# Bucketed attention with a gated feed-forward: the stacked score operands are assembled by compute engines in place of transfers

## The chip, the cores and the metric

The kernel runs on one core of a Trainium2 chip. Time is what the device takes for one execution, in microseconds (us). A core has five engines with a queue each: PE multiplies matrices, DVE, ACT and POOL work on tiles in SBUF (DVE and ACT on PSUM too), SP here only issues transfers. Transfers run on 16 DMA engines; each is issued by an instruction in the queue of SP or ACT, and a queue is worked off in order. The program is built by a scheduler that takes a priority from the kernel's own counter (`at(g, k)`), draws the waits from the tiles, and fixes the order on each engine before anything runs.

## The reference

Four batches with eight heads of 768 positions and 64 channels go through attention in which a query sees only the keys of its own hash bucket (six sign bits of a projection); a gated feed-forward layer over each batch follows.

```python
q_bits = (np.einsum('bhsd,dk->bhsk', q, proj) > 0)      # k_bits alike, from k
q_bucket = np.sum(q_bits * 2 ** np.arange(6), axis=-1)
mask = q_bucket[:, :, :, None] == k_bucket[:, :, None, :]
scores = np.where(mask, np.matmul(q, k.transpose(0, 1, 3, 2)) / 8, -1e9)
attn = softmax(scores);  x = attn @ v
# per batch, x is 768 x 512
h = np.maximum(x @ w_in, 0);  u, v = h[..., :512], h[..., 512:]
v_n = (v - mean(v)) / np.sqrt(var(v) + 1e-6)
out = (u * (w_spatial @ v_n + b_spatial[:, None])) @ w_out
```

## The kernel before, in words

There are 32 heads (n = 0 to 31), handled in pairs (p = n // 2, e = n % 2): a pair's q and k are one tile `qk` of 128 rows, of which head e has rows 64e to 64e + 63. To keep float32's accuracy with float16 matmuls each operand is split into a rounded part and a remainder. `split_qk` makes the tile `hl` (128 x 4 x 768, float16): slot 1 and 2 are the rounded k and q (ACT, line 186), slot 0 and 3 the remainders (DVE, lines 187 and 188). `hash_rows` multiplies q and k with the projection and turns the signs into rows of plus and minus a large number, `sg` (DVE, lines 178 and 180); multiplied with each other these rows add a large negative number to a score whose buckets differ.

A score tile (128 queries by 768 keys, `sp`) is then two matmuls of up to 128 rows for each half of the keys, lines 300 and 301. Their operands are stacked in `ab`, one of four tiles of 128 x 4 x 768 that the heads take in turn: rows 0 to 63 hold the head's parts, rows 64 to 127 the other parts in slots 0 and 1, and the hash rows with zeros in slots 2 and 3. Putting `ab` together is `build(n)`, lines 191 to 217. Since a head's rows have to come to other rows than where `hl` and `sg` hold them, it issues transfers from SBUF to SBUF: four small ones of hash rows (line 203), and one or two of 192 or 384 KB from `hl` (lines 201, 207, 216, 217). For heads 8 to 31 (`near`) two copies by DVE that stay on their rows (lines 209 and 210) stand for part of it, and the four small transfers are issued from ACT's queue.

The main loop runs over g = 6n + i, six score tiles a head. For heads 0 and 8 to 31 a tile goes: matmuls (lines 300 and 301), a pass of DVE that also takes the row maximum (302), ACT's exponent (303, 304), a split of the result into two float16 parts `pp` (ACT 307, DVE or POOL 308), a transposing transfer `pt` issued by SP (310), and 18 matmuls with v (323 to 325), five tiles later. For heads 1 to 7 (`KEYS`) the scores are made with keys and queries exchanged (`scores_k`, lines 269 to 272), which needs the row maxima first (`row_max`, lines 248 to 261) and no transfer per tile; in that time the feed-forward weights are loaded and split too. When the heads of a batch are done, its feed-forward layer is spread over the heads of the next batch in 28 units (lines 372 to 448); the last batch's stands alone at the end.

`build(n + 2)` is called at tile i = 0 of head n. `split_qk(r + 2)` comes at tile 3 of an odd head, where r is the pair that runs; there is one `hl` tile and one `qk` tile at a time, so the next split waits for whatever still reads `hl`, and the next load of `qk` for the split.

## Time and profile before

| | |
|---|---|
| median of 3 runs | 709.54 us (708.9 to 712.29) |
| the profiled execution | 708.95 us, of which its span is 707.2 us |
| granted TensorE clock, mean | 0.964 |
| busy share of the span | PE 87%, DVE 72%, ACT 64%, POOL 31% |
| DMA, mean share of 16 engines | 78%, 111.51 MB moved |

The span is read in five stages: until the first score matmul (0 to 16.5 us), head 0 (to 62), the KEYS heads 1 to 7 (to 175), heads 8 to 31 with the feed-forward layers of three batches (to 632, called the long stage), and the last feed-forward layer (to 707.2). In the profile's rows a name such as `ab<-hl` is output and input of an instruction, `SPq` and `ACTq` are the queues of SP and ACT where they issue transfers, and what stands behind `<-` in brackets is what ended the engine's idle time.

### The profile page before, as it was taken

How to read it: one execution, taken by the hardware profiler on the slowest of the kernel's cores; microseconds unless marked ns; L12 is line 12 of the kernel's file. 1: busy time of each engine (PE TensorE's matmuls, PEld its weight loads, DVE VectorE, ACT ScalarE, POOL GpSimd, SP SyncE). 2: the span in 40 equal slices, each digit the busy share in tenths (PEclk: the TensorE clock that was granted, in tenths of full speed). 3: DMA queues.
4: the chain of work that ended last, by engine and by line, in shares of the span. 5: the costliest groups of instructions: out<-in, count | busy, mean ns of one | idle time of the engine just before them, and what ended most of it. 6: DMA issues, size and time to landing. Idle time of an engine off the chain costs nothing.

```text
span 707.2 us, 14858 instructions
## 1 busy us (share of the span) xinstructions
PE 618.5 (87%) x5735; PEld 391.0 (55%) x5735; DVE 511.3 (72%) x961; ACT 454.2 (64%) x806; POOL 222.0 (31%) x215
## 2 busy tenths in 40 slices
PE   1668798999796989999796999899888999999997
PEld 0236676778453655565454565565445655655553
DVE  4665698388888897779699897899697987725100
ACT  1444477567686868777588786868677688724121
POOL 5111434454324452152002162033022530322513
PEclk9999798699899999999998999999999999999999
DMA  9557557353698979998989999999989899950011
GB/s 242 143 109 185 125 154 161 89 163 106 134 185 176 184 161 199 217 194 192 206 153 214 165 197 191 201 185 215 214 171 151 158 180 206 156 132 1 0 45 45
DMA packets 286555, 111.51 MB, mean 158 GB/s; under 512 B 270356, under 2 KB 273428, under 8 KB 286484
## 3 DMA queue, kind: packets, MB, share of 16 engines
q1 hardware_dynamic: 284180, 109.67, 77.0%
q10 hardware_dynamic: 2304, 0.89, 0.6%
q8 instruction: 45, 0.74, 0.4%
q14 instruction: 26, 0.21, 0.1%
HBM read 28.33 MB, written 6.29 MB: 49 GB/s over the span
## 4 chain that ended last, share of the span: by engine, by line
PE 48%; DMA 22%; DVE 11%; issue 7%; SPq 4%; ACT 4%; POOL 4%; ACTq 0%; DVEq 0%; POOLq 0%
DMA pt<-pp 14%; PE sps L428 7%; PE ops L443 7%; PE vps L372 6%; PE ups L413 6%; PE pv L282 4%; DMA ab<-hl 4%; PE sp L300 3%; PE sp L301 3%; PE pv L323 3%; SPq L310 2%; PE pv L325 2%; PE pv L324 2%; DVE ex L302 2%; PE sp L269 1%
## 5 line engine op out<-in xcount | busy, mean ns | idle before, releaser
L302 DVE TENSOR_SCALAR_CACHE_REDUCE ex<-sp 128x768 f32<-128x768 f32 x150 | 141.8, 951 | 42.1 <-PE sp L301 39.7
L304 ACT ACTIVATE ex<-ex,nb 128x768 f32<-128x768 f32 x150 | 139.3, 932 | 7.4 <-ACT nb L303 4.5
L323 PE MATMUL pv<-vp,pt 128*128 128x65 f16 x900 | 105.7, 196 | 43.3 <-DMA pt<-pp 42.7
L307 ACT CAST pp<-ex 128x768 f16<-128x768 f32 x150 | 123.7, 826 | 10.5 <-DMA pt<-pp 5.2
L308 DVE TENSOR_TENSOR pp<-ex,pp 128x768 f16<-128x768 f32 x116 | 123.1, 1064 | 9.5 <-ACT pp L307 8.9
L308 POOL TENSOR_TENSOR pp<-ex,pp 128x768 f16<-128x768 f32 x34 | 57.9, 1702 | 218.0 <-ACT pp L307 175.3
L323 PEld LDWEIGHTS <-pt 128*128 128x128 f16 x900 | 85.5, 100 | 70.7 <-DMA pt<-pp 61.8
L300 PE MATMUL sp<-ab 128*128 128x384 f16 x300 | 102.1, 340 | 14.4 <-DMA ab<-hl 9.3
L324 PE MATMUL pv<-vp,pt 128*128 128x64 f16 x900 | 105.4, 196 | 0.0
L325 PE MATMUL pv<-vp,pt 128*128 128x65 f16 x900 | 104.8, 197 | 0.0
L301 PE MATMUL sp<-ab 127*128 127x384 f16 (+1 forms) x300 | 102.2, 341 | 0.6 <-DMA ab<-sg 0.6
L428 PE MATMUL sps<-ws,vn 128*128 128x384 f16 x576 | 100.7, 326 | 0.5 <-DVE sy L432 0.5
L324 PEld LDWEIGHTS <-pt 128*128 128x128 f16 x900 | 85.9, 99 | 10.7 <-issue 1.9
L325 PEld LDWEIGHTS <-pt 128*128 128x128 f16 x900 | 86.0, 99 | 2.3 <-issue 0.6
L428 PEld LDWEIGHTS <-vn 128*128 128x128 f16 x576 | 54.3, 98 | 35.1 <-issue 1.8
L282 PEld LDWEIGHTS pv<-vf,ex 128*128 128x128 f32 x504 | 69.2, 210 | 3.2 <-issue 1.0
L372 PE MATMUL vps<-wi,xt 128*128 128x512 f16 x288 | 67.4, 382 | 3.2 <-DMA xt<-xs 3.2
L413 PE MATMUL ups<-xt,wi 128*128 128x384 f16 x384 | 69.4, 333 | 0.0
L443 PE MATMUL ops<-wo,g 128*128 128x512 f16 x288 | 67.8, 379 | 1.0 <-ACT o L447 0.9
L282 PE MATMUL pv<-vf,ex 128*128 128x65 f32 x504 | 68.0, 289 | 0.0
L303 ACT ACTIVATE nb<-mx 128x1 f32<-128x1 f32 x150 | 29.3, 197 | 57.2 <-DVE ex L302 56.2
L433 POOL TENSOR_TENSOR sy<-sy,u 128x384 f32<-128x384 f32 x32 | 35.9, 1125 | 75.5 <-DVE sy L432 54.5
(91 smaller groups left out, 920.8 us busy)
## 6 DMA issues: line engine op xcount, KB each, us to landing
qk<-kq SPq DMA_DIRECT2D x16, 768.0 KB
ab<-hl SPq DMA_DIRECT2D x34, 192.0 KB
out<-o SPq DMA_DIRECT2D x24, 256.0 KB
v<-v SPq DMA_DIRECT2D x13, 384.0 KB
raw<-w_in SPq DMA_DIRECT2D x16, 256.0 KB
ab<-hl SPq DMA_DIRECT2D x7, 384.0 KB
pt<-pp SPq DMA_TRANSPOSE x150
raw<-w_sp SPq DMA_DIRECT2D x12, 192.0 KB
```

What stands on the lines that cost most here:

```text
L282: nc.tensor.matmul(acc[:, qi, :], lhsT=ex[:, qi * P:(qi + 1) * P], rhs=vf[p % 2][:, 2 * i + e, :], start=(i == 0 and qi == 0), stop=(i == ...
L300: nc.tensor.matmul(ps[:, c], lhsT=t[:, 0, qs], rhs=t[:, 1, cs], start=True, stop=False)
L301: nc.tensor.matmul(ps[:, c], lhsT=t[0:K, 3, qs], rhs=t[0:K, 2, cs], start=False, stop=True)
L302: nc.vector.tensor_scalar(ex, ps, -float(2 ** 28), None, op0=ALU.max, op1=ALU.max, accum_out=mx)
L304: st["ex", n, i] = nc.scalar.activation(ex, ex, AF.Exp, bias=nb, scale=ISQ).ins
L307: nc.scalar.copy(pp[:, 0], ex)
L308: (nc.gpsimd if i in (PL_POOL if n >= 2 * NH else PL_POOL1) else nc.vector).tensor_tensor(out=pp[:, 1], in0=ex, in1=pp[:, 0], op=ALU.subtract)
L323: nc.tensor.matmul(acc, lhsT=pt[:, c, :], rhs=vh, start=(i == 0 and c == 0), stop=False)
L324: nc.tensor.matmul(acc[:, 0:D], lhsT=pt[:, c, :], rhs=vl, start=False, stop=False)
L325: nc.tensor.matmul(acc, lhsT=pt[:, NT + c, :], rhs=vh, start=False, stop=(i == NT - 1 and c == NT - 1))
L428: nc.tensor.matmul(ps[:, :HS], lhsT=vn[gv][:, c, d * P:(d + 1) * P], rhs=ws[gw][:, c, hs], start=(k == 0), stop=(k == 3 * NT - 1))
L443: nc.tensor.matmul(ps, lhsT=gt[h][gg][:, c, j * P:(j + 1) * P], rhs=wo[gw][:, c, :], start=(k == 0), stop=(k == 3 * NF - 1))
```

## The change

All transfers in `build` go. `build(n)` now returns four steps, which the loop runs one after the other:

- `codes`: four instructions that take 32 rows of `sg` each, multiply them with a column `hm` of 0 or the head's factor, and write them to rows 64 to 95 of `ab`; two by ACT and two by DVE (head 0: four by ACT). The rows of the pair's other head come along and are zeroed by the factor, so the separate scaling in `hash_rows` (line 180) goes.
- `high` and `cross`: copies of 64 x 1536 float16 from `hl` to rows 0 to 63 and 64 to 127. The one that stays on its rows is POOL's, the one that crosses to the other half DVE's (head 0: ACT and DVE).
- `low`: a third copy of that size, by DVE.

For heads 2 to 7 all four run at tile 0 of head n - 2, for heads 8 to 31 one at each of tiles 0 to 3. At the start `hm` is made from a small tile `hw`, head 1's operands follow head 0's, head 1's row maxima are spread over tiles 0 to 3 of head 0 (so far five came ahead at tile 0 and one at tile 1), and some loads are placed in another order. Heads 9, 11 and so on now stack as the even heads do, with 127 rows in line 301's matmul.

```diff
+    hw = const.tile([P, 2, 4], F32, name="hw")
+    nc.gpsimd.memset(hw, 1.0)
+    nc.gpsimd.affine_select(out=hw, in_=hw, compare_op=ALU.is_ge, fill=0.0, base=0,
+                            pattern=[[-16, 2], [-32, 4]], channel_multiplier=1)
+    nc.gpsimd.affine_select(out=hw, in_=hw, compare_op=ALU.is_ge, fill=0.0, base=15,
+                            pattern=[[16, 2], [32, 4]], channel_multiplier=-1)
...
-        s0 = wk.tile([P, HS], F16, tag="sg0", name=f"sg0_{p}")
+        s0 = wk.tile([P, HS], F16, tag="sg0", bufs=2, name=f"sg0_{p}")
         nc.vector.tensor_scalar(s0, hp[:, :HS], 0.0, hv[:, 0:1], op0=ALU.is_gt, op1=ALU.subtract)
-        s1 = wk.tile([P, HS], F16, tag="sg1", bufs=2, name=f"sg1_{p}")
-        nc.vector.tensor_scalar(s1, s0, hv[:, 1:2], None, op0=ALU.mult)
-        st["sg", p] = s1
+        st["sg", p] = s0
...
-        for j in range(4):
-            q_s.dma_start(
-                out=t[z:z + 2 * NB, 3 - j // 2, (j % 2) * HS:(j % 2 + 1) * HS],
-                in_=sg[32 * j + 16 * e:32 * j + 16 * e + 2 * NB, :])
...
-        q_h.dma_start(out=t[z:z + D, 0:2], in_=hl[r, 2:4])
+        def codes():
+            for j in range(4):
+                js, hs = slice(32 * j, 32 * j + 32), slice((j % 2) * HS, (j % 2 + 1) * HS)
+                to = t[D:D + 32, 3 - j // 2, hs]
+                if j < 2 or n == 0:
+                    st["code"] = nc.scalar.activation(to, sg[js], AF.Copy, scale=hm[js, e:e + 1]).ins
+                else:
+                    nc.vector.tensor_scalar(to, sg[js], hm[js, e:e + 1], None, op0=ALU.mult)
+
+        def high():
+            if n == 0:
+                nc.scalar.copy(t[0:D, 2:4], hl[r, 1:3])
+            else:
+                OWN[e].tensor_copy(t[0:D, 2:4], hl[r, 1:3])
+
+        def low():
+            nc.vector.tensor_copy(t[0:D, 0:2], hl[r, 0:2])
+
+        def cross():
+            eng = nc.vector if n == 0 else OWN[1 - e]
+            st["cross"] = eng.tensor_copy(t[D:P, 0:2], hl[r, 2:4]).ins
+
+        return [codes, high, low, cross]
+
+    OWN = (nc.gpsimd, nc.vector)
...
     nc.sync.dma_start(out=hc, in_=hconst)
     load_qk(0)
+    nc.vector.reduce_sum(hm, hw, axis=AX.X)
+    nc.vector.tensor_scalar(hm, hm, hv[:, 1:2], None, op0=ALU.mult)
     hash_rows(0)
+    at(-40, 1)
     split_qk(0)
-    build(0)
+    at(-39, 0)
+    for part in build(0):
+        part()
+    load_v(0)
+    at(-38, 0)
     load_qk(1)
-    build(1)
-    load_v(0)
+    at(0, 150)
+    first = st["cross"], st["code"]
+    with tc.issue_after(first[0]), tc.issue_after(first[1]):
+        for part in build(1):
+            part()
...
-    rml = [(NT * n + i - NT - LEAD, n, i) for n in sorted(KEYS) for i in range(NT)]
+    rml = [((0, 1, 2, 2, 3, 3)[i] if n == 1 else NT * n + i - NT - LEAD, n, i) for n in sorted(KEYS) for i in range(NT)]
...
-            if i == BI and n + 2 < N:
-                build(n + 2)
+            if i == 0 and n + 2 < N:
+                parts = build(n + 2)
+            for part in parts[:1] if n + 2 >= NH else parts:
+                part()
+                parts = parts[1:]
```

Where the order on an engine moved is shown below at three places. A row is a line of the kernel, an operation, output and input with their numbers, and the output's size.

SP's queue from the start of the program to the first transposing transfer of head 0 (`pt_0`), before the change (`ab_82` is head 0's operand tile, `ab_83` head 1's, `ab_85` head 3's):

```order
L216 DMA ab_83<-hl_121 64x2x1536
L217 DMA ab_82<-hl_121 64x1536
L150 DMA qk_132<-kq 128x1536
L217 DMA ab_83<-hl_121 64x1536
L203 DMA ab_82<-sg_0_119 12x384 x4
L203 DMA ab_83<-sg_0_119 12x384 x4
L156 DMA v_4_1201<-v 128x768
L216 DMA ab_85<-hl_167 64x2x1536
L150 DMA qk_173<-kq 128x1536
L203 DMA ab_85<-sg_1_165 12x384 x4
L217 DMA ab_85<-hl_167 64x1536
L310 DMA_TRANSPOSE pt_0_156<-pp_0_153 128x12x128
```

The same stretch of SP's queue with the change (lines are numbered higher by 7 or 8 there, and L505 on is the start):

```order
L131 DMA bt<-b_sp 128x768
L157 DMA qk_139<-kq 128x1536
L163 DMA v_4_1207<-v 128x768
L157 DMA qk_177<-kq 128x1536
L318 DMA_TRANSPOSE pt_0_162<-pp_0_159 128x12x128
L318 DMA_TRANSPOSE pt_1_205<-pp_1_202 128x12x128
```

Only loads are left ahead of `pt_0`; SP holds 270 rows in place of 322, and ACT issues no transfer any more.

DVE's queue from the signs of pair 0 to head 0's first score tiles (`ex_0`, `ex_1`), before:

```order
L178 TENSOR_SCALAR sg_0_117<-hp_112,hc 128x384
L224 SCALAR_TENSOR_TENSOR vp_94<-v_0_140,vp_94 128x12x64
L180 TENSOR_SCALAR sg_0_119<-sg_0_117,hc 128x384
L178 TENSOR_SCALAR sg_1_163<-hp_158,hc 128x384
L187 SCALAR_TENSOR_TENSOR hl_167<-qk_132,hl_167 128x768
L188 SCALAR_TENSOR_TENSOR hl_167<-qk_132,hl_167 128x768
L180 TENSOR_SCALAR sg_1_165<-sg_1_163,hc 128x384
L302 TENSOR_SCALAR ex_0_144,mx_143<-sp_0_145 128x768
L250 TENSOR_REDUCE mx_177<-mp_0_178 128x1
```

DVE's queue at that place with the change (`ab_87` is head 0's operand tile, `ab_88` head 1's):

```order
L185 TENSOR_SCALAR sg_0_124<-hp_119,hc 128x384
L217 COPY ab_87<-hl_126 64x1536
L221 COPY ab_87<-hl_126 64x1536
L214 COPY ab_88<-hl_126 64x1536
L217 COPY ab_88<-hl_126 64x1536
L208 TENSOR_SCALAR ab_88<-sg_0_124,hm 32x384 x2
L310 TENSOR_SCALAR ex_0_150,mx_149<-sp_0_151 128x768
L258 TENSOR_REDUCE mx_181<-mp_0_182 128x1
L232 SCALAR_TENSOR_TENSOR vp_99<-v_0_137,vp_99 128x12x64
L310 TENSOR_SCALAR ex_1_193,mx_149<-sp_1_194 128x768
L185 TENSOR_SCALAR sg_1_169<-hp_164,hc 128x384
```

The split and signs of pair 1, which stood ahead of `ex_0`, now stand behind `ex_1`; copies and codes of heads 0 and 1 have come in ahead of `ex_0`.

POOL's queue around heads 17 to 19, in the long stage, before (`pp_2` is the second part of a head's tile 2, `vn` belongs to a feed-forward layer):

```order
L308 TENSOR_TENSOR pp_2_4280<-ex_2_4271,pp_2_4280 128x768
L308 TENSOR_TENSOR pp_2_4577<-ex_2_4568,pp_2_4577 128x768
L401 TENSOR_TENSOR vn_1_4123<-vr_0_4172,vn_0_4122 128x512
L401 TENSOR_TENSOR vn_1_4123<-vr_1_4266,vn_0_4122 128x512
L401 TENSOR_TENSOR vn_1_4123<-vr_2_4361,vn_0_4122 128x512
L308 TENSOR_TENSOR pp_2_4870<-ex_2_4861,pp_2_4870 128x768
```

POOL's queue there with the change:

```order
L214 COPY ab_87<-hl_4316 64x1536
L316 TENSOR_TENSOR pp_2_4270<-ex_2_4261,pp_2_4270 128x768
L221 COPY ab_88<-hl_4316 64x1536
L316 TENSOR_TENSOR pp_2_4565<-ex_2_4556,pp_2_4565 128x768
L409 TENSOR_TENSOR vn_1_4115<-vr_0_4164,vn_0_4114 128x512
L409 TENSOR_TENSOR vn_1_4115<-vr_1_4256,vn_0_4114 128x512
L409 TENSOR_TENSOR vn_1_4115<-vr_2_4351,vn_0_4114 128x512
L316 TENSOR_TENSOR pp_2_4858<-ex_2_4849,pp_2_4858 128x768
L214 COPY ab_89<-hl_4904 64x1536
L221 COPY ab_90<-hl_4904 64x1536
```

Two copies a pair have come in between POOL's other work, here for heads 20 and 21 (`ab_87`, `ab_88`) and for heads 22 and 23.

29 lines of the change are left out of this document (6 added, 23 removed).

## The prediction, made before the changed kernel ran

> **What bounds the kernel now.** I read the page first, then the busy time by stage: the five stages, and one 60 us piece of the long stage.
>
> ```profile
> span 707.2 us, 14858 instructions
> PE 618.5 (87%) x5735; PEld 391.0 (55%) x5735; DVE 511.3 (72%) x961; ACT 454.2 (64%) x806; POOL 222.0 (31%) x215
> ...
> 0.00:16.50 16.50, 1.52 (x9) 0.25 (x9) 7.67 (x9) 3.50 (x3) 9.80 (x19) 1.00 0.96 231
> 16.50:62.00 45.50, 30.44 (x203) 15.96 (x204) 26.95 (x40) 17.66 (x27) 5.92 (x9) 1.00 0.68 151
> 62.00:175.00 113.00, 104.03 (x727) 83.71 (x727) 84.37 (x178) 74.12 (x145) 48.77 (x64) 0.88 0.49 133
> 175.00:632.00 457.00, 412.12 (x4416) 253.82 (x4415) 378.57 (x701) 339.73 (x595) 135.52 (x102) 0.97 0.97 183
> 632.00:707.20 75.20, 70.42 (x384) 37.26 (x382) 13.71 (x34) 19.20 (x39) 22.00 (x22) 1.00 0.09 29
> ...
> 360.00:420.00 60.00, 51.66 (x555) 32.31 (x553) 54.48 (x105) 45.47 (x84) 15.10 (x12) 0.91 0.98 180
> ```
>
> Behind a stage's length stand the busy times of PE, PEld, DVE, ACT and POOL, then the granted clock, the DMA engines' share and GB/s. The last stage is PE alone and holds no `build`. In the long stage PE is busy 412 of 457 us, so 45 us are all that can be won there; DVE with 379 (83%; 91% in the piece from 360) and DMA with a share of 0.97 stand close behind it. In the KEYS stage PE is busy 104 of 113 at a clock of 0.88. In the first 62 us PE is idle for 30. Next, who keeps PE waiting: PE's waits in the long stage, the chain's shares there, ACT's waits there, and PE's waits in the KEYS stage.
>
> ```profile
> PE pv L323 <- DMA pt<-pp: 36.6, 32, 3.2
> PE sp L300 <- DVE ex L302: 3.8, 7, 0.9
> ...
> by line: DMA pt<-pp 20.4%; PE ops L443 7.6%; issue 7.4%; PE sps L428 5.7%; PE ups L413 5.7%; PE vps L372 5.4%; PE sp L300 4.9%; PE sp L301 4.7%; PE pv L323 3.8%; DMA ab<-hl 3.4%; PE pv L325 3.2%; PE pv L324 3.1%; SPq L310 2.8%; DVE ex L302
> ...
> ACT hl L186 <- DMA ab<-hl: 8.3, 7, 2.0
> ...
> PE sp L269 <- ACT ex L272: 6.1, 5, 3.7
> ```
>
> Of PE's 45 idle us, 37 are waits for a transposed tile `pt`; that transfer is also the largest link of the chain, 20.4% of this window or 93 us. So the long stage is paced by the row DVE, ACT, DVE or POOL, SP, DMA, PE, with PE near its limit and the transposing transfers late. The transfers of `build` take part with 3.4% (16 us): ACT may not overwrite `hl` before they have read it.
>
> **The start.** These are rows of the timeline, and the first piece of the chain:
>
> ```profile
> 1.19 4.39 DMA qk<-kq
> ...
> 5.61 1.48 ACT L186 ACTIVATE hl<-qk 128x1536 f16<-128x1536 f32 x1 [3.60 <-DMA qk<-kq]
> 8.57 1.20 DVE L188 SCALAR_TENSOR_TENSOR hl<-qk,hl 128x768 f16<-128x768 f32 x1
> 10.59 1.37 SPq L150 DMA_DIRECT2D qk<-kq  x1
> 16.49 0.50 PE L300 MATMUL sp<-ab 128*128 128x384 f16 x1 [9.27 <-DMA ab<-hl]
> 18.48 1.51 PE L173 MATMUL hp<-qk,hc 128*32 128x384 f32 x8 [1.49 <-DMA qk<-kq]
> 20.60 0.48 PE L301 MATMUL sp<-ab 127*128 127x384 f16 x1 [0.61 <-DMA ab<-sg]
> 23.62 0.95 DVE L302 TENSOR_SCALAR_CACHE_REDUCE ex<-sp 128x768 f32<-128x768 f32 x1
> 28.39 1.60 SPq L310 DMA_TRANSPOSE pt<-pp  x1
> 48.76 0.96 DVE L302 TENSOR_SCALAR_CACHE_REDUCE ex<-sp 128x768 f32<-128x768 f32 x1 [0.46 <-PE sp L301]
> ```
>
> The first score matmul waits for transfers until 16.49, its partner until 20.60, and `ex` of tile 0 starts at 23.62, tile 5's at 48.76. What the engines will need instead goes by these rows (minimum, median and maximum of a line in ns where three numbers stand; else mean):
>
> ```profile
> L209 DVE COPY ab<-hl x24: 540/554/1420, 127.6 to 551.0; 64x1536 f16<-64x1536 f16 x24
> L178 DVE TENSOR_SCALAR sg<-hp,hc x16: 596/610/619, 9.7 to 545.7; 128x384 f16<-128x384 f32 x16
> L180 DVE TENSOR_SCALAR sg<-sg,hc x16: 301/318/1781, 11.1 to 546.4; 128x384 f16<-128x384 f16 x16
> L349 ACT CAST xs<-x 128x384 f16<-128x384 f32 x32 | 16.0, 501 | 2.5 <-POOL x L342 1.4 <-DVE x L344 0.7 <-issue 0.2
> L250 DVE TENSOR_REDUCE mx<-mp 128x1 f32<-128x768 f32 x42 | 39.8, 952 | 18.2 <-PE mp L248 17.8
> L85 POOL MEMSET ab<- 64x1536 f16 x2 | 2.7, 1376 | 0.1
> L308 POOL TENSOR_TENSOR pp<-ex,pp x34: 1634/1647/2453, 26.7 to 612.5; 128x768 f16<-128x768 f32 x34
> ```
>
> With the change: the split of pair 0 ends at 8.57 + 1.20 = 9.8, the signs take 0.6 more (10.4), `low` and `cross` 2 x 0.55 (11.5). ACT's four codes have the length of L349's 384 elements, 0.50 each: 10.4 + 2.0 = 12.4; `high` by ACT, about L186's 1.48 (7.1 to 8.6), lies ahead of them. The matmuls behind the last code lead to a full tile about 1.1 us later, 13.5; DVE is through head 1's two copies and two codes at 11.5 + 1.1 + 0.6 = 13.2. So `ex` of tile 0 starts near 13.5, 10 us earlier. Not all of it is kept. The load of pair 1's qk leaves after the split as now, and took 7.9 us from issue to use (18.48 less 10.59) beside the five transfers of lines 201 to 217 for heads 0 and 1 (1.2 MB), 4.4 when first in line; I take landing at 16, in place of 18.4. DVE's work in its new order from the end of `ex` 0 up to `ex` 5 is nine maxima, five passes, four remainders, two `pp` and a split of v, all of 128 x 768 (21 x 0.95, the length of L250 and L302), six copies (3.3), four codes (1.3), signs and small ones (1.4), together 26 us: 14.5 + 26 = 40.5, or 42.5 where it waits for pair 1. Against 48.76 that is 6 to 8 us; I take **-7** (bounds -3, if the loads land no earlier than now, and -10, the first tile's full gain).
>
> **The KEYS stage.** Heads 3 to 9 are built here: ten more copies on DVE (5.5 us) and fourteen codes (4.5), fourteen codes on ACT (7), seven copies on POOL. DVE has 113 - 84 idle, ACT 39, POOL 64, and PE is the limit, so their cover is PE's own 104 us; without it the price is DVE's 10. Removed is the place where ACT waits for `hl`: one stall of PE on `ex` of 3.7 us (the 6.1 above, longest 3.7) hangs on it. I take **-3**, bounds -5 and +4 (a copy of POOL ahead of `x` or of a weight's remainder).
>
> **The long stage.** Removed from SP and ACT, by these rows of the tile `ab`, of the DMA view and of the transposing issue:
>
> ```profile
> L217 SPq DMA_DIRECT2D ab<-hl x32: 462/865/1644, 10.0 to 578.9; - x32
> L203 ACTq DMA_DIRECT2D ab<-sg x96: 727/736/1569, 149.9 to 574.1; - x96
> L310 SPq DMA_TRANSPOSE pt<-pp x150: 1307/1657/3611, 28.4 to 621.3; - x150
> ...
> DMA packets 254165, 83.57 MB, mean 183 GB/s; under 512 B 246911, under 2 KB 247967, under 8 KB 254111
> ab<-hl SPq DMA_DIRECT2D x22, 192.0 KB
> ab<-sg ACTq DMA_DIRECT2D x88, 9.0 KB
> ```
>
> 22 transfers of 192 KB are 4.3 of 83.6 MB, with the small ones 6%: the DMA share falls from 0.97 to about 0.91. SP has 22 x 0.87 = 19 us of issuing less ahead of transposes of 1.66 each; ACT's queue 88 x 0.74 = 65, much of it under ACT's own running work. The 8.3 us in which ACT waits to overwrite `hl` shrink, since the copies follow the split and not SP's queue. Of the 93 us that the chain spends on `pt` 6% is 6; of its 16 us on `ab<-hl` I count 6 as won, since a chain that loses a link goes on by the next one. Together -12, a third of PE's 37.
>
> Added to DVE: two codes a head for the 22 heads built here, 44 x 0.32 = 14, less the scaling of L180 (10 x 0.32 = 3); the copies stay two a head. To ACT 44 x 0.50 = 22, in place of the 65 of issuing. To POOL 22 copies. No row shows such a copy; it is bounded by the memset of the same tile size that only writes (1.38) and by twice the two-input pass of half its length (3.3), and being one input and one output in float16 it is nearest to the memset: 1.5, 33 us together, on an engine busy 30%. But DVE and POOL get in each other's way: L209's median of 0.55 goes to 1.42, L180's 0.32 to 1.78. If a third of POOL's added time falls on DVE, that is 11 more; DVE then holds 379 + 11 + 11 = 401. Behind a blocked DVE instruction stand the passes of the next scores and `pp`, for which SP's transposes wait. At the 91% that DVE reached, 401 need 441 us, still under 457 - 8. The page's part 4 has DVE with 11% of the chain:
>
> ```profile
> PE 48%; DMA 22%; DVE 11%; issue 7%; SPq 4%; ACT 4%; POOL 4%; ACTq 0%; DVEq 0%; POOLq 0%
> ```
>
> 22 x 0.11 = 2.4 is the least that DVE's added time costs; for what queues behind it I take **+4**, and have **-8** net (bounds -27 and +20, from the rivals below).
>
> Sum: 708.95 (span 707.2, and 1.75 around it) - 7 - 3 - 8 = **691**. The median of the runs is 0.6 above the profiled one, less than a measurement can tell.
>
> **Rivals.** *DMA is the limit.* For it: the share of 0.97, and `pt` as PE's one big wait. Then the long stage shrinks by all of the 6%, 457 x 0.06 = 27, and ends at PE 412 of 430; with the start and KEYS 708.95 - 10 - 27 = 672. Against it: shares over a whole stage at 0.97 with PE at 90% at once look like overlapping packets.
>
> *The start's gain is taken back.* The KEYS stage is PE at a clock of 0.88, and an earlier, denser start can bring more half-clocked time; ten earlier us then become waits for weights and clock, and the long stage gains nothing as DVE's added work eats SP's relief: some 4 us of the three terms' 18 are left, 705.
>
> *POOL blocks DVE.* The copies start when the split is done, just when DVE runs the remainders and its own copies of the same `hl`; each holds DVE up for its whole length. The Trainium skill, "SBUF — State Buffer", section "SBUF: two separate sides", says that GpSimd and a VectorE instruction in a two-port mode, or with two SBUF inputs, exclude each other for the whole instruction; by that rule this rival is the likelier, and the maxima of L209 and L180 above agree with it, while their medians show that most instructions escape. At 2.0 us a copy, DVE holds 379 + 11 + 44 = 434, at 91% 477 us: +20, with the -10 of the start and KEYS that is 719. It decides from DVE's 416 (91% of 457) on, which is 1.2 us lost a copy.
>
> That the change does not do what it says is out: no `ab<-hl` or `ab<-sg` stands in either queue any more.
>
> **How the numbers follow.** The forecast, 691 with 682 to 700 as its own range, has 0.53; DMA as the limit 0.17; the gain taken back 0.15; POOL blocking DVE 0.15. A measurement tells 0.5% (3.5 us) from no change, so faster is under 706 and slower over 713. Faster: 0.53 + 0.17 + half of the gain taken back (0.07) = 0.77; same 0.10; slower 0.13. The range of 8 in 10 reaches from 668, a little under the DMA rival, to 710, past the gain taken back; it leaves out POOL blocking DVE and the tail of the first, 0.18 together.
>
> **What would show it.** Right: `ex` of tile 0 near 13.5 and of tile 5 near 41; no ACT wait for `hl` on a DMA; PE's waits for `pt` in the long stage near 25; POOL's copy near 1.5; DVE near 400 busy there. Wrong: a POOL copy over 2 us or L209's successors at a median of 1 us or more, with PE waiting for `pp` as SP does now; a granted clock in KEYS under 0.85; or waits for `pt` still at 35, which would say that neither SP's queue nor the DMA load made them late.

## The result: slower by 4.5%

The changed kernel takes 741.95 us (median of 4 runs, 741.58 to 742.03), the kernel before 709.56 (708.90 to 712.29) on the same chip: a ratio of 1.0448, with a 95% interval of 1.042 to 1.0475. The forecast was 691, a gain of 18 us; it is a loss of 32. These are lines of the page of the changed kernel, in the order in which those of the kernel before were shown (its line numbers are some 8 higher: the pass `ex` is L310, `pp` L316, the score matmuls L308 and L309, the first `pv` matmul L331):

```profile
span 740.2 us, 14795 instructions
PE 629.2 (85%) x5735; PEld 395.3 (53%) x5735; DVE 585.5 (79%) x1025; ACT 495.4 (67%) x873; POOL 280.4 (38%) x247
...
PE 36%; DVE 31%; DMA 13%; issue 9%; ACT 8%; POOL 2%; SPq 1%; DVEq 0%; ACTq 0%; POOLq 0%
...
L308 PE MATMUL sp<-ab 128*128 128x384 f16 x300 | 105.5, 352 | 37.5 <-DVE ex L310 29.2
L331 PE MATMUL pv<-vp,pt 128*128 128x65 f16 x900 | 109.7, 200 | 29.1 <-DMA pt<-pp 28.9
```

VectorE's share of the chain goes from 11% to 31%, and what PE now waits for as long as for the transposes is VectorE's pass `ex`. The busy times by stage (PE, PEld, DVE, ACT, POOL; then the granted clock, the DMA share, GB/s):

```profile
12.00:60.00 48.00, 30.78 (x212) 16.65 (x213) 41.66 (x65) 25.16 (x42) 13.52 (x14) 0.79 0.46 109
60.00:175.00 115.00, 102.56 (x767) 81.43 (x766) 96.75 (x179) 75.90 (x141) 56.97 (x65) 0.96 0.37 108
175.00:632.00 457.00, 391.45 (x4006) 238.95 (x4005) 406.66 (x707) 351.08 (x618) 167.38 (x116) 0.92 0.84 160
632.00:740.20 108.20, 102.89 (x744) 58.04 (x744) 32.41 (x68) 37.77 (x71) 32.03 (x31) 1.00 0.33 68
```

PE's waits in the long stage (us in total, times, longest):

```profile
PE pv L331 <- DMA pt<-pp: 27.1, 16, 3.8
PE sp L308 <- DVE ex L310: 26.2, 21, 3.6
```

The DMA share fell from 0.97 to 0.84 and the waits for `pt` from 36.6 to 27.1 us, the share lower than the forecast's 0.91, the waits near its 25. The waits for `ex` rose from 3.8 to 26.2. The stage is not over at 632: the clean measure is the stretch of equal work, from the first pass of head 8 to the first pass of head 31. It begins at 178.3 us before and at 171.5 now, and it took 424.8 and takes 464.1. So in these two executions the start and the KEYS stage together won 7 us, and the long stage lost 39. The work is equal but for some weight preparation of VectorE, which lies ahead of the stretch before (0.8 us in it) and partly in it now (12.1 us, lines 144 to 147). A stretch comes from one execution of a kernel, and executions of one kernel lie up to 10 us apart (the kernel before 703 to 713 us beside e1 below), so a few us between two stretches say nothing by themselves. For e4 and e8 the profiled execution was among the slower ones, and no stretch is given for them. The same stretch in both kernels, before first:

```profile
178.30:603.10 424.80, 379.96 (x4077) 233.07 (x4077) 358.86 (x667) 323.91 (x567) 123.68 (x91) 0.97 0.99 185
```

```profile
171.50:635.60 464.10, 397.06 (x4059) 242.32 (x4059) 412.38 (x718) 356.82 (x627) 168.04 (x116) 0.92 0.83 160
```

VectorE is busy 53.5 us longer there, where the forecast had 22 more. Where these come from, the lines of the tiles `hl` and `ab` show (minimum, median and maximum of one instruction in ns):

```profile
L192 DVE SCALAR_TENSOR_TENSOR hl<-qk,hl x16: 944/959/2980, 7.0 to 575.2; 128x768 f16<-128x768 f32 x16
L193 DVE SCALAR_TENSOR_TENSOR hl<-qk,hl x16: 944/1078/4773, 8.6 to 576.1; 128x768 f16<-128x768 f32 x16
L217 DVE COPY ab<-hl x32: 539/556/2145, 10.6 to 581.5; 64x1536 f16<-64x1536 f16 x32
L221 POOL COPY ab<-hl x16: 1462/1716/2512, 10.2 to 577.2; 64x1536 f16<-64x1536 f16 x16
L214 POOL COPY ab<-hl x15: 1457/1490/2267, 18.6 to 572.5; 64x1536 f16<-64x1536 f16 x15
L208 DVE TENSOR_SCALAR ab<-sg,hm x62: 309/318/1611, 14.3 to 574.3; 32x384 f16<-32x384 f16 x62
L206 ACT ACTIVATE ab<-sg,hm x66: 608/612/614, 10.8 to 608.8; 32x384 f16<-32x384 f16 x66
```

The medians are near the forecast's rows, but for ScalarE's code (0.61 us for 0.50); VectorE's maxima are three to five times its medians. One such place, in the timeline of VectorE, then of GpSimd, ScalarE and PE (start, length, instruction; in brackets the idle time before it):

```profile
282.79 1.52 DVE L192 SCALAR_TENSOR_TENSOR hl<-qk,hl 128x768 f16<-128x768 f32 x1
284.24 4.68 DVE L193 SCALAR_TENSOR_TENSOR hl<-qk,hl 128x768 f16<-128x768 f32 x1
288.84 1.26 DVE L217 COPY ab<-hl 64x1536 f16<-64x1536 f16 x1
290.03 0.94 DVE L310 TENSOR_SCALAR_CACHE_REDUCE ex<-sp 128x768 f32<-128x768 f32 x1
...
283.45 2.19 POOL L214 COPY ab<-hl 64x1536 f16<-64x1536 f16 x1
285.60 0.91 POOL L443 TENSOR_TENSOR g<-sy,g 128x384 f16<-128x384 f32 x1
286.47 1.63 POOL L316 TENSOR_TENSOR pp<-ex,pp 128x768 f16<-128x768 f32 x1
288.07 1.62 POOL L443 TENSOR_TENSOR g<-sy,g 128x384 f16<-128x384 f32 x1
...
291.01 0.20 ACT L311 ACTIVATE nb<-mx 128x1 f32<-128x1 f32 x1 [6.70 <-DVE ex L310]
...
291.03 0.48 PE L308 MATMUL sp<-ab 128*128 128x384 f16 x1 [3.57 <-DVE ex L310]
```

A remainder of 0.95 us takes 4.68: it runs beside GpSimd's copy and beside what GpSimd runs straight after it, and ends in the course of the fourth. The pass `ex` stands behind it on VectorE, ScalarE stands 6.70 us for that pass, and PE 3.57.

In what follows, the *excess* of VectorE is the sum, over its instructions, of the time above a quick one of the same line and shape (the tenth percentile). In the stretch it is 25 us before and 63 in the changed kernel. Of the 63, 60 lie on instructions that ran beside one of GpSimd's (22 of the 25 before); and of GpSimd's 20 copies there 19 ran beside a VectorE instruction that took over 0.1 us longer than a quick one. That GpSimd's own long copies keep others waiting is out: neither ScalarE, to overwrite `hl`, nor PE, for `ab`, waits for one of them in the stretch.

### The profile page after: what moved, and what is told of

Same layout as the page of the kernel before. It is cut to its first block, busy times and chain, and to the rows that moved or that the text cites. A ratio compares the mean times of both kernels' runs of the same rounds, so it can differ in the third digit from the quotient of the medians.

```text
span 740.2 us, 14795 instructions
## 1 busy us (share of the span) xinstructions
PE 629.2 (85%) x5735; PEld 395.3 (53%) x5735; DVE 585.5 (79%) x1025; ACT 495.4 (67%) x873; POOL 280.4 (38%) x247
## 4 chain that ended last, share of the span: by engine, by line
PE 36%; DVE 31%; DMA 13%; issue 9%; ACT 8%; POOL 2%; SPq 1%; DVEq 0%; ACTq 0%; POOLq 0%
DMA pt<-pp 8%; PE sps L436 7%; PE ops L451 6%; DVE ex L310 5%; DVE pp L316 5%; DVE hl L193 3%; PE pv L290 3%; PE ups L421 3%; PE vps L380 3%; DVE ab L208 3%; DVE ab L217 2%; PE sp L308 2%; PE sp L309 2%; DMA xt<-xs 2%; DVE mx L258 2%
## 5 line engine op out<-in xcount | busy, mean ns | idle before, releaser
L310 DVE TENSOR_SCALAR_CACHE_REDUCE ex<-sp 128x768 f32<-128x768 f32 x150 | 141.2, 949 | 23.0 <-PE sp L309 20.6
L316 DVE TENSOR_TENSOR pp<-ex,pp 128x768 f16<-128x768 f32 x116 | 125.7, 1086 | 15.5 <-ACT pp L315 15.0
L308 PE MATMUL sp<-ab 128*128 128x384 f16 x300 | 105.5, 352 | 37.5 <-DVE ex L310 29.2
L331 PE MATMUL pv<-vp,pt 128*128 128x65 f16 x900 | 109.7, 200 | 29.1 <-DMA pt<-pp 28.9
L331 PEld LDWEIGHTS <-pt 128*128 128x128 f16 x900 | 88.8, 103 | 51.9 <-DMA pt<-pp 38.7
L316 POOL TENSOR_TENSOR pp<-ex,pp 128x768 f16<-128x768 f32 x34 | 59.4, 1747 | 147.3 <-ACT pp L315 94.2
L333 PE MATMUL pv<-vp,pt 128*128 128x65 f16 x900 | 108.8, 201 | 0.0
L332 PE MATMUL pv<-vp,pt 128*128 128x64 f16 x900 | 108.7, 199 | 0.0
L309 PE MATMUL sp<-ab 127*128 127x384 f16 x300 | 106.6, 355 | 0.0
L332 PEld LDWEIGHTS <-pt 128*128 128x128 f16 x900 | 88.5, 102 | 10.5 <-issue 2.0
L333 PEld LDWEIGHTS <-pt 128*128 128x128 f16 x900 | 88.3, 102 | 4.0 <-issue 1.8
L436 PEld LDWEIGHTS <-vn 128*128 128x128 f16 x576 | 54.8, 98 | 40.3 <-issue 4.0
L380 PE MATMUL vps<-wi,xt 128*128 128x512 f16 x288 | 69.1, 389 | 4.7 <-DVE sg L185 2.4
L451 PE MATMUL ops<-wo,g 128*128 128x512 f16 x288 | 70.3, 388 | 1.4 <-ACT o L455 1.4
L290 PEld LDWEIGHTS pv<-vf,ex 128*128 128x128 f32 x504 | 64.5, 198 | 3.0 <-issue 0.5
L290 PE MATMUL pv<-vf,ex 128*128 128x65 f32 x504 | 63.5, 277 | 0.0
```

The costliest lines, as they stand in the source:

```text
L290: nc.tensor.matmul(acc[:, qi, :], lhsT=ex[:, qi * P:(qi + 1) * P], rhs=vf[p % 2][:, 2 * i + e, :], start=(i == 0 and qi == 0), stop=(i == ...
L308: nc.tensor.matmul(ps[:, c], lhsT=t[:, 0, qs], rhs=t[:, 1, cs], start=True, stop=False)
L309: nc.tensor.matmul(ps[:, c], lhsT=t[0:K, 3, qs], rhs=t[0:K, 2, cs], start=False, stop=True)
L310: nc.vector.tensor_scalar(ex, ps, -float(2 ** 28), None, op0=ALU.max, op1=ALU.max, accum_out=mx)
L316: (nc.gpsimd if i in (PL_POOL if n >= 2 * NH else PL_POOL1) else nc.vector).tensor_tensor(out=pp[:, 1], in0=ex, in1=pp[:, 0], op=ALU.subtract)
L331: nc.tensor.matmul(acc, lhsT=pt[:, c, :], rhs=vh, start=(i == 0 and c == 0), stop=False)
```

## The experiments

All runs in one table. The ratio is to the kernel before, run beside it on the same chip; "stretch" goes from the first pass of head 8 to that of head 31 in the profiled execution, with VectorE's busy time and the DMA share in it.

| run | ratio (95%) | stretch, us | VectorE busy | DMA |
|---|---|---|---|---|
| before | 1 | 424.8 | 358.9 | 0.99 |
| the change | 1.0448 (1.042 to 1.0475) | 464.1 | 412.4 | 0.83 |
| e1: GpSimd's copies by VectorE | 1.0162 (1.0113 to 1.0211) | 445.5 | 389.7 | 0.88 |
| e2: GpSimd's copies by ScalarE | 1.0139 (1.0078 to 1.0200) | 436.3 | 379.1 | 0.92 |
| e3: before, one copy by GpSimd | 1.0110 (1.0037 to 1.0183) | 436.6 | 376.3 | 0.94 |
| e4: engines for heads 0 to 7 only | 0.9930 (0.9871 to 0.9988) | | | |
| e5: e1, codes by transfer from head 8 | 0.9873 (0.9830 to 0.9916) | 426.3 | 377.9 | 0.93 |
| e6: e1, `cross` by transfer from head 8 | 1.0126 (1.0079 to 1.0173) | 441.4 | 377.6 | 0.95 |
| e7: the change, GpSimd's copies twice | 1.1220 (1.1173 to 1.1266) | 503.9 | 431.8 | 0.78 |
| e8: e4 with all copies by VectorE | 0.9857 (0.9815 to 0.9898) | | | |
| e9: e5, VectorE's codes by VectorE | 1.0297 (1.0180 to 1.0413) | 449.3 | 397.2 | 0.86 |
| e10: e5, ScalarE's codes by ScalarE | 0.9975 (0.9920 to 1.0029) | 428.9 | 374.9 | 0.91 |
| e11: the change, GpSimd's copies as float32 | 1.0070 (1.0032 to 1.0107) | 442.8 | 392.0 | 0.89 |
| e12: e1, VectorE's codes twice | 1.0241 (1.0181 to 1.0301) | 452.9 | 399.9 | 0.85 |
| e13: e5, `cross` by ScalarE as float32 | 0.9793 (0.9757 to 0.9828) | 421.1 | 362.1 | 0.95 |
| e14: e5, VectorE's copies as float32 | 0.9882 (0.9844 to 0.9920) | 427.6 | 376.7 | 0.93 |

### Who makes the copy: e1 and e2

```diff
-    OWN = (nc.gpsimd, nc.vector)
+    OWN = (nc.vector, nc.vector)                           # e1
+    OWN = (nc.scalar.copy, nc.vector.tensor_copy)          # e2, with the calls to match
```

> The changed kernel, with the copies that it gives to GpSimd (`high` or `cross`, one a head from head 1 on) given to VectorE instead. Everything else stays. Theory (GpSimd blocks VectorE): VectorE gains 22 copies of 0.55 us, 12 us, in the long stage and loses about 37 us of held-up time, the excess over a line's quick instructions there going from 63 back to the 27 of the kernel before; VectorE's busy time in 175 to 632 us falls from 407 to about 382, PE's waits for `ex` (L308, 25.8 us in 175 to 660) fall under 10, and the time falls from 742 to about 717 (710 to 725). Rival (VectorE simply has too much to do, codes and copies, and whatever it is given lengthens the path): its busy time grows to about 415 and the time is 745 to 755. Rival (the order of the work or the clock, not the copies): within 738 to 746, with PE's waits for `ex` unchanged.

> The changed kernel, with GpSimd's copies given to ScalarE, which shows no slower instruction anywhere when GpSimd runs; its own copy of this size took 1.47 us at the start, so it is given 22 x 1.47 = 32 us in the long stage, on 351 that it was busy there. Theory (GpSimd blocks VectorE): VectorE's excess over its quick instructions falls from 63 to about 27 us, VectorE to about 370 busy, and what ACT's new work costs stands against it: 715 to 735, under the 742 of the changed kernel. Rival (the engine that makes the copy doesn't matter, the added work or the order does): 742 or more, with PE's waits for `ex` unchanged or longer.

Both come out at 1.015, where the change has 1.045: two thirds of the loss hang on the 31 copies being GpSimd's. In e1 VectorE has 20 copies *more* in the stretch, 11 us, and is busy 23 us *less*; 10 us of that are weight preparation that lies ahead of the stretch again (2.0 us in it), the others come from shorter instructions. The groups of VectorE there (busy us, mean ns), the change first, then e1:

```profile
L208 DVE TENSOR_SCALAR ab<-sg,hm 32x384 f16<-32x384 f16 x40 | 20.7, 517 | 1.0
L193 DVE SCALAR_TENSOR_TENSOR hl<-qk,hl 128x768 f16<-128x768 f32 x10 | 19.8, 1976 | 0.0
L217 DVE COPY ab<-hl 64x1536 f16<-64x1536 f16 x20 | 16.1, 804 | 0.2
```

```profile
L193 DVE SCALAR_TENSOR_TENSOR hl<-qk,hl 128x768 f16<-128x768 f32 x10 | 16.8, 1682 | 0.0
L208 DVE TENSOR_SCALAR ab<-sg,hm 32x384 f16<-32x384 f16 x40 | 14.7, 368 | 0.9
L217 DVE COPY ab<-hl 64x1536 f16<-64x1536 f16 x20 | 11.7, 586 | 0.2
```

The same instructions, in the same numbers, are 6, 3 and 4.4 us shorter. The excess falls from 63 to 36 us. Two signs of the theory were missed: the excess was to go back to 27, and PE's waits for `ex`, which were to fall under 10 us, are 18.2. The rivals (VectorE has too much to do already; the order or the clock) asked for 738 or more in e1. They fall for this part; e2's further rival, that it does not matter which engine copies, too. But a third of the loss is left in e1, and 20 us in its stretch.

### GpSimd's copy alone, and its dose: e3, e7, e11

e3 is the kernel before with one line changed, so nothing of the change is in it:

```diff
-            nc.vector.tensor_copy(t[r, 2:4], hl[r, 1:3])
+            nc.gpsimd.tensor_copy(t[r, 2:4], hl[r, 1:3])
```

> The kernel before, with one of the two copies that VectorE makes for each of heads 8 to 31 (L209) given to GpSimd; nothing else changes: VectorE has 24 x 0.55 = 13 us less to do, GpSimd some 24 x 1.5 = 36 us more, the transfers stay. Theory (GpSimd's copies block VectorE by themselves): VectorE's excess grows by 24 x 1.2 to 1.7 us, its busy time in the long stage rises from 379 to 395 or so in spite of the copies taken from it, and the time goes from 709.6 to 718 to 732. Rival (the loss comes from the work and the order that the change adds to VectorE and ScalarE): 703 to 711, as VectorE has less to do.

VectorE has less to do and the kernel is 1.1% slower; the stretch is 12 us longer and VectorE busier by 17, with the excess at 43 in place of 25. The time is just under the expectation of 718 to 732 (717 on the scale of 709.6), and the interval reaches down to 1.0037. Of the 17 us, some 10 are weight preparation that falls into the stretch here.

e7 issues each of GpSimd's copies twice; e11 writes the same bytes as half as many elements:

```diff
-                OWN[e].tensor_copy(t[0:D, 2:4], hl[r, 1:3])
+                for _ in range(2 - e):                                                    # e7
+                    OWN[e].tensor_copy(t[0:D, 2:4], hl[r, 1:3])
+                mv(OWN[e], t[0:D, 2:4], hl[r, 1:3])                                       # e11
...
+    def mv(eng, to, src):
+        if eng is nc.gpsimd:
+            to, src = to.bitcast(F32), src.bitcast(F32)
+        return eng.tensor_copy(to, src)
```

`cross` is edited in the same way.

> The changed kernel with each of GpSimd's copies made twice: GpSimd has 31 x 1.5 = 46 us more, 22 of the copies in the long stage, 33 us; nobody else has more to do, GpSimd is then busy some 200 of 457 there. Theory (the time in which GpSimd copies is time in which VectorE's two-port instructions stand): the excess of VectorE over its quick instructions in the long stage goes from 63 to about 95 us, and the time from 742 to 755 to 775. Rival (it is the place of the copy in the order, not its length): 742 to 750. Rival (GpSimd's copies cost nothing, their run with VectorE was chance): within 3 us of 742.

> The changed kernel, with GpSimd's copies of 64 x 1536 float16 written as 64 x 768 float32 over the same bytes. If GpSimd's time goes by elements, a copy takes about 0.75 us in place of 1.46 to 1.72; if by bytes, it stays. Theory (VectorE stands for as long as GpSimd copies): with half the length about half of what the copies cost goes, and the time is 727 to 734 where the changed kernel took 742 and e1, without GpSimd's copies, 720; the excess of VectorE in the long stage falls from 63 to about 47. Rival (each copy costs by its start and its place in the order, not by its length): 740 or more, though the copies are shorter. If the copies aren't shorter the run tells nothing and is within 3 us of 742.

```profile
L230 POOL COPY ab<-hl x31: 816/852/1551, 10.4 to 549.7; 64x768 f32<-64x768 f32 x31
```

GpSimd's copy goes by elements: a median of 0.85 us, about half. The ratio goes with the time that GpSimd copies in the whole program: 1.007 with 30 us, 1.045 with 53, 1.122 with 108, which is 27 us of time for 23 of copying and 55 for 55. That is more than the expectations in both directions: 714 instead of 727 to 734, and 796 instead of 755 to 775. The excess, which e11 was to bring to 47, explains only part: 46, 63 and 76 us for stretches of 443, 464 and 504. In e7 PE waited 63 us for `ex`:

```profile
PE sp L310 <- DVE ex L312: 63.1, 35, 6.0
PE pv L333 <- DMA pt<-pp: 24.6, 19, 7.3
```

Single waits are up to 6 us long, as one held-up instruction lets the passes, the exponentials and the scores behind it stand in a row. That a hold costs more than its length for this reason fits the rows, but no run takes it apart from the clock, which is granted at 0.91 in e7's stretch, 0.92 in the change's and 0.97 before.

### What is left in e1: e5, e6, e9, e10

From head 8 on, e5 brings the hash rows by four small transfers as before the change, all copies staying on VectorE; e6 keeps the codes on the engines and brings `cross` by a transfer:

```diff
+                    nc.scalar.dma_start(                                                   # e5
+                        out=t[z:z + 2 * NB, 3 - j // 2, hs],
+                        in_=sg[32 * j + 16 * e:32 * j + 16 * e + 2 * NB, :])
...
+                nc.sync.dma_start(out=t[z:z + D, 0:2], in_=hl[r, 2:4])                     # e6
```

> As e1 (all copies by VectorE), but from head 8 on the hash rows come by four small transfers on ACT's queue, from signs scaled by VectorE, as before the change; the three copies a head stay on VectorE. Against e1 VectorE has 14 - 3 = 11 us less to do in the long stage and ACT 27 us of code work less, against 65 us of issuing. From the first pass of head 8 to the first of head 31 the kernel before took 425 us, the changed one 464, e1 445. Theory (VectorE's added work is on the path nearly at its full length: e1's 12 us of copies more than e2's cost 9): 435 there, and the time 7 to 12 us under e1's, 709 to 714. Rival (ACT's code work, which stands behind the exponentials, is what is left of the loss): 427 there, 703. Rival (neither; the order of the parts or the start costs it): 443 to 447, as e1.

> As e1, but from head 8 on the copy across the halves is one transfer of 192 KB on SP's queue, as before the change; codes by ScalarE and VectorE as in the change. Against e1 VectorE has 12 us less to do in the long stage, SP 19 us of issuing more, the DMA engines 4.3 MB more. Theory (VectorE's added work is on the path): 435 from the first pass of head 8 to that of head 31, the time 709 to 714. Rival (ACT's code work is what is left of the loss): 445 there or a little less, as e1. Rival (the transfer returns what it cost before, by SP's queue and DMA): 445 or more.

e5 wins all that was left of the loss, and the start's gain besides: 0.987, the stretch at 426. That is the number of its rival (ScalarE's codes, 427) and not of its theory (435); e9 and e10 below tell which work it was. e6 wins next to nothing on e1 (1.0126 and 1.0162, and the intervals overlap), though VectorE has as little to do as in e5. PE's two largest waits in the stretch, in e5, then in e6:

```profile
PE pv L363 <- DMA pt<-pp: 32.9, 32, 2.9
PE sp L340 <- DVE ex L342: 7.4, 10, 3.0
...
PE pv L363 <- DMA pt<-pp: 33.0, 31, 2.3
PE sp L340 <- DVE ex L342: 17.6, 11, 3.5
```

The waits for `pt` are the same in both, so e6's third expectation, that the transfer brings back what it cost, does not show where it should. What e6 has more than e5 are waits for VectorE's pass `ex`, as many as e1 (18.2 us); and what e1 and e6 have in common are the codes by engines.

e9 and e10 split the codes: from head 8 on only VectorE's two of a head by engine, or only ScalarE's two.

```diff
-                if True:
+                if not (j >= 2):        # e9: VectorE's two codes by engine;  e10: j < 2, ScalarE's two
                     nc.scalar.dma_start(
```

> As e5 (all copies by VectorE, codes by transfer from head 8 on, 426 us from the first pass of head 8 to that of head 31, 697 in all), but VectorE makes its two codes a head itself, as in the change; only the two of ScalarE still come by transfer. VectorE has 44 x 0.32 = 14 us more in the long stage, ACT's queue half of its 65 us of issuing. e1, with all four codes by engines, took 445 there. Theory (what is left of the loss is ScalarE's codes, since taking 12 us of copies from VectorE in e6 gave only 3): 426 to 430, the time 697 to 701. Rival (VectorE's work, a fuller VectorE makes the passes late): 438 to 445, 709 to 716. Rival (half by each): near 435, 707.

> As e5, but ScalarE makes its two codes a head itself, as in the change; the two of VectorE come by transfer. ScalarE has 44 x 0.61 = 27 us more in the long stage, for half of the 65 us of issuing on its queue. Theory (ScalarE's codes are what is left of the loss): 438 to 445 us from the first pass of head 8 to that of head 31, the time 709 to 716. Rival (VectorE's codes): 426 to 430, 697 to 701. Rival (half by each): near 435, 707.

In both, the transferred and the computed hash rows of odd heads lie 16 rows apart, so the hash term is left out of the scores of odd heads from 9 on; the instructions and their sizes are the ones named. The theory (ScalarE's codes) fell. VectorE's 40 codes of a quick 0.32 us, 13 us, lengthen the stretch from 426 to 449, more than even the rival said; ScalarE's 40 of 0.61, 24 us, only to 429, as the rival said. The rest of e10's distance to e5, 1% in all, lies ahead of the stretch (its first pass of head 8 is at 171.2 us, e5's at 165.0). VectorE is busy 19 us longer in e9 than in e5: 13 of codes and 7 of excess (41 in place of 34). So of the 39 us that the change loses in the stretch 19 go with GpSimd's copies (464 to 445 in e1) and 19 with the codes (445 to 426 in e5), by e9 and e10 VectorE's two of a head.

### VectorE's load as such: e12, e13, e14

e12 makes VectorE's codes of e1 twice; e13 gives `cross` of e5 to ScalarE, e14 writes VectorE's copies of e5 as float32:

```diff
-                    nc.vector.tensor_scalar(to, sg[js], hm[js, e:e + 1], None, op0=ALU.mult)
+                    for _ in range(2 if n >= NH else 1):                                               # e12
+                        nc.vector.tensor_scalar(to, sg[js], hm[js, e:e + 1], None, op0=ALU.mult)
...
-                nc.vector.tensor_copy(t[z:z + D, 0:2], hl[r, 2:4])
+                nc.scalar.copy(t[z:z + D, 0:2].bitcast(F32), hl[r, 2:4].bitcast(F32))                  # e13
+                nc.vector.tensor_copy(t[z:z + D, 0:2].bitcast(F32), hl[r, 2:4].bitcast(F32))           # e14, and the two others
```

> As e1 (all copies by VectorE, no copy by GpSimd), with VectorE's two codes of each head from 8 on made twice: 44 x 0.32 = 14 us more for VectorE in the long stage, nothing for anyone else. So far the stretch from the first pass of head 8 to that of head 31 goes with VectorE's busy time in it: 379 gave 436, 390 gave 445, 397 gave 449, 412 gave 464, while 359 to 378 gave 425 to 429. Theory (over about 378 VectorE is the limit, each us more on it costs one): VectorE 404 to 410 there, the stretch 457 to 463, the time 731 to 738. Rival (the codes cost by where they stand, before an exponential's partner, and a second one right behind the first costs little): the stretch 445 to 450, 719 to 724.

> As e5 (codes by transfer from head 8 on), with the copy across the halves by ScalarE, written as 64 x 768 float32 over the same bytes, in place of VectorE: VectorE 12 us less in the long stage, ScalarE 22 copies of some 0.8 us more, 18 us on 326. Theory (VectorE is the limit only above about 378, and e5 is just there): 366 on VectorE, the stretch 420 to 426, the time 690 to 697, 0.977 to 0.987 of the kernel before. Rival (ScalarE, which makes the exponentials, becomes the bound): over 430, over 700.

> As e5, with VectorE's three copies a head, from head 8 on, written as 64 x 768 float32 over the same bytes. Either VectorE's copy goes by bytes, then it stays near 0.55 us and the time is e5's, 697; or by elements, then it is near 0.3, VectorE has 16 us less to do and the time is 690 to 697; or it gets slower, 0.85, VectorE has 20 us more, 398 in the stretch, and by the theory (VectorE is the limit above 378) that is 450 and 721; by the rival (VectorE's work isn't what sets the end) it stays under 705.

The stretch in e12, then in e13:

```profile
171.00:623.90 452.90, 389.13 (x4058) 235.90 (x4057) 399.93 (x760) 351.69 (x613) 131.56 (x92) 0.95 0.85 162
```

```profile
167.00:588.10 421.10, 380.07 (x4072) 232.81 (x4072) 362.05 (x672) 342.07 (x591) 125.41 (x92) 0.96 0.95 177
```

Its copies by ScalarE:

```profile
L253 ACT COPY ab<-hl x24: 829/830/835, 144.4 to 566.1; 64x768 f32<-64x768 f32 x24
```

In e12 VectorE's 10 us more go with 7.4 more in the stretch, between the two expectations; but the profiled execution (730.3 us) is its slowest of four, the ratios of e12 and e1 are only 5.6 us apart on the scale of 709.6, and their intervals overlap. Set beside e9, where 13 us of codes made the stretch 23 longer, the same amount of work has two prices, so its length alone does not set them.

Side by side, the kernels with VectorE at 390 to 412 us have it busy for 0.875 to 0.889 of the stretch, whatever it does there (389.7/445.5, 392.0/442.8, 397.2/449.3, 399.9/452.9, 412.4/464.1). That looks like a limit at some 0.88 of its time, but does not show one: e5 has 0.886 at a stretch of 426, e7 only 0.857 with VectorE at 432 us, and e3 and e6 take 437 and 441 with no more on VectorE than e5 (376 to 378). VectorE's busy time also holds its own hold-ups. What can be said is that a fuller VectorE went with a longer stretch, and that no kernel had it above 0.89. e13, where VectorE is at 362, is the fastest kernel of all: 692.96 us, 0.979 of the kernel before, 0.976 to 0.983; PE waits 28.6 us for `pt` and 9.3 for `ex` there. VectorE's copy in e14 keeps its 0.55 us as float32 (it goes by bytes), so e14 only repeats e5, and does.

### Where the start's gain stayed: e4 and e8

```diff
+        return [codes, high, low, cross] if n < NE else [sent]    # NE = 8; sent: the build before the change; e8: all copies by VectorE
```

> Heads 0 to 7 are assembled as in the change (codes by ScalarE and VectorE, copies by VectorE and GpSimd, the start's new order), heads 8 to 31 as in the kernel before (signs scaled by VectorE, four small transfers, one transfer of 192 KB, two VectorE copies). Theory (the start and the KEYS stage won 7 us, all of the loss lies in the assembly of heads 10 to 31 in the long stage): the last head's first pass, at 603 before and 636 after, is near 596, and the time is 702 (698 to 706). Rival (the gained start brings more half-clocked PE time, and is given back later whatever is done there): 707 to 713. Rival (the new order of the schedule costs the long stage by itself): over 715.

> As e4 (heads 0 to 7 assembled by engines, heads 8 to 31 by transfers as in the kernel before), with GpSimd's copies of heads 1 to 7 given to VectorE, which in the first 175 us has idle time. e4 came out at 0.993 of the kernel before (0.987 to 0.999). Theory (GpSimd's copies hold up VectorE at the start and in the KEYS stage too): 1 to 4 us under e4, 698 to 702 on the scale where before is 707.6, a ratio of 0.988. Rival (VectorE is the bound of the start, and its own copies cost what the held-up time cost): as e4, 0.993. Rival (the gain of the start is lost behind it, e4's gain was scatter): 0.998 to 1.002.

With the long stage put back, the start and the KEYS stage alone give 0.993, and 0.986 without GpSimd's copies. The intervals overlap (0.987 to 0.990), so that GpSimd's copies cost something at the start too is likely and not shown. That the gain is given back later, or that the new order costs by itself, is out for e8, whose interval ends at 0.990.

## Why the prediction failed, step by step

**The start, -7: the mechanism right, the size about half.** `ex` of tile 0 starts at 14.97 (forecast 13.5, before 23.62), tile 5's at 44.93 (41; 48.76): 3.8 us won by then. The mis-sized terms: a code of ScalarE takes 0.61 us where the cast of 384 elements gave 0.50, and GpSimd's copy of head 1 falls on the very instructions that tile 0 needs:

```profile
10.18 1.46 POOL L221 COPY ab<-hl 64x1536 f16<-64x1536 f16 x1
10.58 1.47 DVE L217 COPY ab<-hl 64x1536 f16<-64x1536 f16 x1
10.76 3.78 ACT L206 ACTIVATE ab<-sg,hm 32x384 f16<-32x384 f16 x6 [2.32 <-DVE sg L185]
12.08 1.10 DVE L221 COPY ab<-hl 64x1536 f16<-64x1536 f16 x1
```

These two copies of VectorE take 2.57 us for 1.10; the first score matmul waits for the second of them, till 13.24. In e1, without GpSimd's copy, it starts at 12.03 and `ex` of tile 0 at 14.20.

**KEYS, -3: the number met, by another mechanism.** From tile 5's pass of head 0 to the first pass of head 8 in both kernels, before first, with the new wait in the changed one:

```profile
48.80:178.30 129.50, 116.09 (x844) 92.15 (x843) 94.47 (x195) 79.85 (x153) 51.04 (x67) 0.89 0.54 143
44.90:171.50 126.60, 113.17 (x840) 88.78 (x840) 103.21 (x190) 80.24 (x148) 57.45 (x67) 0.93 0.40 113
...
PE mp L256 <- DVE mx L258: 6.8, 5, 1.8
```

PE's waits for ScalarE's `ex` fell from 6.1 us to 1.4, as the term asked, but its waits for VectorE's row maxima `mx` rose from 0.6 to 9.1 (6.8 here, 2.3 at the scores), so PE is idle for 13.4 us in both. The 2.9 us are PE's own busy time, at a granted clock of 0.93 in place of 0.89. In e3, whose KEYS heads are those of the kernel before, the same piece takes 124.7 us: the 2.9 are within what one execution differs from another, and the term was met by luck.

**The relief of SP, ACT and DMA, -12: its sign came true, its mechanism isn't borne out.** PE's waits for `pt` fell to 27.1, near the 25 named. But they do not go with the transfers. These are PE's waits in the stretch of e3, which has all transfers of the kernel before, then of e2, which has none of `build`'s:

```profile
PE pv L323 <- DMA pt<-pp: 26.3, 26, 2.1
PE sp L300 <- DVE ex L302: 21.3, 20, 3.0
...
PE pv L331 <- DMA pt<-pp: 36.5, 31, 2.3
PE sp L308 <- DVE ex L310: 11.9, 11, 3.1
```

The waits fell where the transfers stayed, and stayed where the transfers went. What goes with the stretch is the sum of both waits: 40.4 us before (424.8), 47.6 in e3 (436.6), 48.4 in e2 (436.3), 55.8 in the change (464.1), 40.3 in e5 (426.3), 37.9 in e13 (421.1). So the fall of the one in the change was PE standing for `ex` instead, and no gain. No run shows the 12 us: the best stretch, e13's, is 4 shorter than before, with the four small transfers back and the DMA share at 0.95. Whether the relief is worth anything beside a VectorE that isn't held up stays open.

**DVE's price, +4: the step that failed.** It was to cover 11 us of VectorE's codes and 11 of hold-ups, and what queues behind. In its place the runs show some 38: 19 by GpSimd's copies (e1) and 19 by the codes (e5), by e9 and e10 VectorE's. Three numbers of it were wrong. The first was "if a third of POOL's added time falls on DVE, that is 11 more". The excess rises by 38 us in the stretch; 27 of them went with the 20 copies in e1, three quarters of these copies' 35 us. The other 11 are there without any copy of GpSimd's, 7 of them on the remainders of `split_qk`; in e1 33 of the 36 us lie beside GpSimd's other work. The rest of VectorE's 53.5 is the 9.5 us of codes, as forecast, and some 6 us of weight preparation that slid from the KEYS stage into the stretch. The second was the price of those codes, which the chain's 11% put at a few us: 13 us of them made e9's stretch 23 longer than e5's. The third was the ceiling: "at the 91% that DVE reached" came from one piece of 60 us, and over the stretch VectorE doesn't get past 0.89 in any of the kernels. With 0.885 the forecast's own 401 would have needed 453 of 457 us, half of the gain of 8; this is an estimate, since no run shows 0.885 to be a limit.

**GpSimd's copy at 1.5: nearly right** (medians 1.49 and 1.72, 1.46 at the least). The figure that mattered was the other one, what it does to its neighbour. **The signs** named for being right came near true: `pt` at 27, the copy at 1.49, VectorE at 407 us in the long stage; of those for being wrong only the first showed, in single copies of GpSimd over 2 us (2.51 at most), while KEYS had a clock of 0.96 and L217 a median of 0.56 us. They watched medians and PE's wait for `pt`, and the loss lay in single long instructions and in PE's wait for `ex`.

**The rivals.** "POOL blocks DVE" named the right cause, at 0.15; its sum was wrong in both directions. It took 2.0 us lost a copy, where e1 gives some 1.3 (27 us over 20 copies, past its own point of decision, 1.2), and its 719 is still too low by 23, as it has VectorE's codes at their length alone. The medians of L209 and L180 had been read as "most instructions escape"; but in the long stage of the kernel before only 3 of 21 copies of L209 ran beside GpSimd at all (0.56, 0.54 and 1.42 us), and the change puts GpSimd's copy beside VectorE's work on the same `hl`. By the Trainium skill, "SBUF — State Buffer", section "SBUF: two separate sides", GpSimd and a VectorE instruction in a two-port mode or with two SBUF inputs exclude each other for the whole instruction. The rows agree as far as they go: VectorE's two-input remainders stand (L193 1.98 us in the mean, 0.95 quick), and the pass `ex`, which reads PSUM, keeps its mean of 949 ns. The hold goes further than one instruction, though: 4.68 us beside four of GpSimd's. "DMA is the limit" fell: DMA is at 0.83 and the kernel slower. "The start's gain is taken back" (705) fell with e8, whose interval ends at 0.990 (702 us); e4's alone, to 0.9988, would not decide it.

**What stays open.** PE's own busy time in the stretch rose from 380 to 397 at a clock of 0.92 instead of 0.97. Whether the lower clock only follows from PE's stalls or costs on its own was not taken apart. Why VectorE's codes cost more than their length in e9 and less in e12, by their place in the order or by VectorE's load, is open too.

## What to carry to other kernels

Before work is given to an idle GpSimd, look at what VectorE does in the same microseconds: a copy that waits for the same tile as VectorE's own ran beside VectorE's work on it in 17 of 20 cases here, and a median from places where the two rarely meet says nothing of that. When one wait shrinks, add up all waits of that engine before it is called a gain: here PE stood for another tile instead. Read how full an engine gets from a whole stage, not from its fullest piece. And price an engine's copy by what it counts in: GpSimd and ScalarE copied the same bytes in little more than half the time when they were written as float32, VectorE in the same time.

## What was not expected of the hardware

- A VectorE instruction that has met GpSimd can stay held beyond the instruction it met: 4.68 us for 0.95, beside a copy and three more of GpSimd's instructions back to back. Why it isn't served between two of them no run shows.
- The copy of 64 x 1536 float16 against 64 x 768 float32 over the same bytes: GpSimd 1.49 to 1.72 and 0.85 us, ScalarE 1.47 and 0.83, VectorE 0.55 and 0.55.
- ScalarE's scaled copy of 32 x 384 takes 0.61 us, more than its cast of 128 x 384 (0.50).
- 31 copies of some 1.7 us on an engine that was busy for 31% of the span cost 20 us more than the same copies on VectorE, which was at 83% of the long stage.
